# State chain in one operation over all heads, y products with 64 output rows, and the first two triangular systems by halves

## The chip, the cores and the metric

The kernel runs on one core of a Trainium2 chip. The core has a matrix engine (TensorE, PE in the profile), a vector engine (VectorE, DVE), an activation engine (ScalarE, ACT), a general engine (GpSimd, POOL), and SyncE (SP), which here issues the DMAs. PE writes to eight PSUM banks; DVE and ACT read PSUM, POOL does not. The metric is the time of one launch in device microseconds. All data are 32-bit floats.

## The reference

The first part is a linear recurrence with a matrix state per batch and head (4 batches, 8 heads, 768 time steps, head size 40); the second is a soft mixture of experts over its output. Cut to what matters:

```python
for t in range(768):                       # state: (4, 8, 40, 40), from zero
    y[:, :, t] = einsum('bhd,bhde->bhe', r_t, state)
    Sa    = einsum('bhde,bhe->bhd', state, a_t)
    state = state * w_t[:, :, None, :] - einsum('bhd,bhe->bhde', Sa, b_t)
    state = state + einsum('bhd,bhe->bhde', v_t, k_t)
x = y as (3072, 320)
logits = x @ phi                           # 32 slots, 4 for each of 8 experts
d = softmax(logits, over tokens);  c = softmax(logits, over slots)
slot_out[e] = relu((d.T @ x)[e] @ w1[e]) @ w2[e]      # 320 -> 1024 -> 320
out = c @ slot_out
```

## The kernel before

Time is cut into 12 steps of 64 time steps (`st`, `NST`), and each step into two halves of 32 (`q`). Two steps are a super-step (`ss`, 6 of them). The 8 heads lie in three groups (`u`; 3, 3 and 2 heads, so 120, 120 and 80 partitions), and each group has the 4 batches. Inside a half the recurrence is a triangular system of size 32 for each batch and head; its inverse T is worked out for a whole super-step at once, for the 4 halves, 4 batches and 8 heads: 128 systems, one on each partition after a transpose.

- **Preparation** of a step: `scan_s`, `scan_k`, `scan_c` build running products of w (scans on DVE, 1.8 us each) and scale k, b and a (three wide multiplies of 768 columns, in most steps on POOL); `bda_at` lays out the scaled a by heads; `lgram` makes the entries of the triangular systems (tile `lls`), `gram` the products for the chain (`qls`, `q0s`), `kbtok` and `ctok_of` transposes.
- **Solve** of a super-step: `solve_in` transposes the systems on DVE into `lt_a` and copies them to `n_a` on ACT; `solve_step`, 30 times, is a multiply into a temporary (`tmp_r`) and an addition into `n_a`; `solve_out` transposes `n_a` on DVE into T (`tts`, of which there is one tile; `lt_a` and `n_a` exist once too). `JP` splits the columns between POOL (up to `JP[ss]`) and DVE (the rest): 3 of 32 on POOL in super-step 0, 7 in super-step 1, all on POOL in the other four.
- **Chain** of a step, the part that is sequential from step to step: `chain_g` (products with the state and with v, or with the first half's result; copied from PSUM to `gss` by ACT), `chain_u` (T times G, negated by ACT into `vus`), for each half and each group; then `chain_s`, the new state.
- **Output** of a step, one step later: `y_vut`, `y_sd` (transposes), `y_p` (masked products), `y_y` (the y products, in 32 output rows each, and the multiply into `xs`), then the slot logits and sums (`slots_*`) every second step, and after the last step the experts.

The order of the work is not the order of the calls. Each call is recorded by `Plan` as an operation with its engine and the tiles it touches; consecutive matmuls into one bank with one tiling become one operation. `schedule` gives each a priority (the longest path behind it, moved by 300 times an entry of the string `SHIFT`) and places operations one after the other on the engines by assumed costs; the program is emitted in that order. Where a gap on PE of over 900 ns is expected, `filler` puts dummy matmuls into it (lines 553 and 557), which keep PE busy. `WIN`, `WIN0` and `PRO` give the order in which the calls of a step are recorded. In the trace, all instructions but the fillers carry line 1276, or 1528 and 1534 at both ends.

Of the kernel before, what the change touches and what calls it, by code (L numbers as in the profile page):

```python
# [11 lines left out]
ALU = mybir.AluOpType  # L12
# [17 lines left out]
JP = (3, 7, 32, 32, 32, 32)  # L30
# [80 lines left out]
class Engine:  # L111
# [29 lines left out]
    r"To')E:@oFhXL;s4JO+UO>!OQ!i0IXai!OO0zcwufU0#!2HOO,:!JPOTvYRS|N~[;tR7NkW~!7z]u2Hzu_O&B|%~!R_gLQOXOS#!OF|CO:H6NNQ!c"  # L141
    r"ODIObM^(|f7M#|a+&lAQ<1-Z60-(A]6YO!EM[#!OI!!!$!#OO#!+YTRGu^N+SIK!PECP.mgSdK{<yxftQMI[RFN$cD7-|4S/LM1R+OwvOqe9|kP$"
    r"FvkOTj>[OLqOrEXsRUU|KFO!NE]-$|NSOOT7?vIB|[spk!6FXGAd<QOD$OOHXBnJEI[Z?<ZrP?|2~F|U7O%FS$NgPEV~eAgQ6K9|R65%3|OMI[_C"
    r"OJH|S*DdXv|EN<tC<]P1N|NxRh=B>$XXr|nF){JO:Yk!|z#&.TT^#P#*LVf2^OVkQQ@LHjy!qZN!7G|eoPJ7b|!!$$!!$$!!^R8NjMO(JaXVdP]x"
    r"S]OBHQ!5JCD]=<!h<+Md~%KR:DOH!|oPv-HbO.!TSS9-OQ?IF*4nsN!>;NV!:[|$@H?>RON8OH0a4%|^|[|SQ6SAI/jWMUJ+a|]dCfp3QBOBr!$N"
    r"Ol|7O_xO!vNOS]c?MdO3Oxz*#{zSHPY|D%L~IYP%_9-P<y@OuO,U_4&/7W917HEPwuBs$yhxybQ5iAPyL_P<N#QKNB93#O~EU]@UEiy|$~ea2t:>"
    r".1K|NhE|O|!M.R<z|uRj8Q:l###[UkC!O%[O|J|sOmx~UUQ##cdNl~|W{bkHwH#!P:w#<UX?pNb||JTHQ|MtJ]D09PKK%U#!HlpYOO@K!mMFOqG`"
    r"oJ{LLP!GP/ZOQqH|KOybssS'!NFG!O#!!HON41c!!!=2:+&Rn|e|9YRA{AOnS=Rvi~!#IAE%M)I!DcSZd|esTEecD0N:|On~###xM|J|X|5|>Ow*"
    r"Q'RZO/|M|OV$UOfOjefV%Q[P|oO##|9G5(R.UaP4NGdOvK_PYMMgKLRE'|OOF([OOD|#DPSRN[|<1zjQzQ?ZA|XOVY|O|j]lzMlO7SO@+&MH*;3W"
    r",VH+.4c4F>bup,KU7HD0r!=!OH9qp?uaMyK`{7g{ADgUOO#`UwLj|NrNVGbLP|[7|NOZ;!d%{a~i/YQZeOO2/QwORQczKq3J/G;_Jc!;I@ITTF(C"  # L150
    r"HU(k!~!?&04G#=#_F>vH!H!XPGj,?|OUOdg]de_Y!BLOXmO[A%!Lb0JgW7V))6TO|QOQA#vM!8&rBOxzO90Q|||zp~XhOur|S|J!{T:=PsM+SOZ6"
    r"jKKD+k||NaKF~k]_X]!G6*9P$OB538'F$M3Rhc=#+KOfOuJQwOq7ppOPOTJ:n@jOLLOQg[-Dm%OfC|.O7K#<X$!!VMJO0;@XfdOO2GQo!O'PqZoe"
# [28 lines left out]
class Plan:  # L181
# [34 lines left out]
    def record(self, eng, method, a, k):  # L216
# [7 lines left out]
        if eng == "PE" and self.open is not None:  # L224
            o = self.open
            if o.mode == mode and isinstance(out, VAP) and (o.banks == {out.bank} or self.gather and o.gather) and o.tag == self.tag:
                new = False
        if new:
            o = Op()
            o.eng, o.calls, o.acc, o.banks, o.mode, o.kind, o.dma, o.tag, o.alt = eng, [], {}, set(), mode, method, 0, self.tag, None  # L230
# [7 lines left out]
        for i, x in enumerate(aps):  # L238
            w = i == 0
            if isinstance(x, VAP):  # L240
                if x.bank not in o.banks:
                    o.banks.add(x.bank)
                    x.bank.ops.append(o)
# [417 lines left out]
def rwkv_softmoe(ctx, tc, kb, b2, aa, ww, rr, vv, vq, consts, phi, w1, w2, out):  # L661
# [78 lines left out]
    with ExitStack() as ac:  # L740
# [27 lines left out]
        gss = Ring(part(4, 120) for _ in range(4))  # L768
# [22 lines left out]
        xts = Ring(mid[:, 4 * HD + 512 * i:4 * HD + 512 * i + 512] for i in range(2))  # L791
        wts_t = Ring(space(512) for _ in range(2))
# [17 lines left out]
        def cols(u):  # L810

            return slice(u * 480, u * 480 + 4 * NHU[u] * D)

        def grp(u, b):
            o = u * 480 + b * NHU[u] * D
            return slice(o, o + NHU[u] * D)

# [71 lines left out]
        def kbtok(st, u):  # L889
# [7 lines left out]
            nc.scalar.copy(kbks[st][:, cols(u)], tp[:, 0:4 * n])  # L897
# [66 lines left out]
        def solve_step(ss, i):  # L964
# [573 lines left out]
```

## Time and profile before

| what | value |
|---|---|
| time, median of 3 runs | 428.48 us (427.35 to 433.18) |
| profiled execution, its own time | 428.65 us |
| its span, from first to last instruction | 426.9 us |
| granted TensorE clock, mean | 0.972 |
| busy: PE / DVE / ACT / POOL | 365.3 / 261.7 / 221.6 / 246.7 us |
| weight loads (PEld) | 312.1 us |
| matmul instructions | 9473 |
| DMA traffic | 59.33 MB, mean 139 GB/s |

PE's busy time counts dummy matmuls as well. A matmul of 32-bit floats is two instructions (with two weight loads), so counts in the trace are twice those of calls in the code. Because nearly all instructions share one line, groups are told apart by engine, operation, tiles and shapes: `32*32 32x40` is a product with 32 contracted rows, 32 output rows and 40 columns (U and G of the chain), `128*32 128x40` the y products, `120*128 120x192` those of `y_p`; a `128xN` TENSOR_TENSOR from `wt` to `wt` is a solve step, one of `120x768` a multiply of the preparation.

### The profile page before, as it was taken

How to read it: one execution, taken by the hardware profiler on the slowest of the kernel's cores; microseconds unless marked ns; L12 is line 12 of the kernel's file. 1: busy time of each engine (PE TensorE's matmuls, PEld its weight loads, DVE VectorE, ACT ScalarE, POOL GpSimd, SP SyncE). 2: the span in 40 equal slices, each digit the busy share in tenths (PEclk: the TensorE clock that was granted, in tenths of full speed). 3: DMA queues.
4: the chain of work that ended last, by engine and by line, in shares of the span. 5: the costliest groups of instructions: out<-in, count | busy, mean ns of one | idle time of the engine just before them, and what ended most of it. 6: DMA issues, size and time to landing. Idle time of an engine off the chain costs nothing.

```text
span 426.9 us, 21521 instructions
## 1 busy us (share of the span) xinstructions
PE 365.3 (86%) x9473; PEld 312.1 (73%) x9473; DVE 261.7 (61%) x558; ACT 221.6 (52%) x637; POOL 246.7 (58%) x410
## 2 busy tenths in 40 slices
PE   0598996899999998899997999999979889889930
PEld 0587985799978897677896889987868778734830
DVE  6689989799958448854597644735542534642130
ACT  1550544964357654977437566597544266522130
POOL 6457964958499999889978899288820000110000
PEclk9999999999999999999998999999989999989985
DMA  8989232134222444404353324387675465881077
GB/s 197 248 221 271 59 81 60 55 101 128 77 77 76 133 123 129 128 19 137 89 177 102 100 68 114 103 259 245 185 213 162 132 174 175 245 257 64 3 174 195
DMA packets 36894, 59.33 MB, mean 139 GB/s; under 512 B 4849, under 2 KB 26465, under 8 KB 36801
## 3 DMA queue, kind: packets, MB, share of 16 engines
q1 hardware_dynamic: 36801, 57.96, 48.0%
q8 instruction: 74, 1.21, 1.2%
q14 instruction: 19, 0.16, 0.1%
HBM read 54.01 MB, written 3.93 MB: 136 GB/s over the span
## 4 chain that ended last, share of the span: by engine, by line
PE 60%; DVE 11%; ACT 8%; POOL 7%; issue 7%; DMA 3%; SPq 1%; DVEq 0%; ACTq 0%
PE ps L1276 53%; DVE wt L1276 9%; POOL wt L1276 7%; ACT wt L1276 5%; PE ps L557 4%; DMA bm_t<-in_consts_dram 2%; PE ps L553 2%; ACT mem L1276 2%; DMA mem<-in_rr_dram 1%; SPq L1276 1%; DVE mem L1276 1%; DVE old L1276 0%; DVE ps L1276 0%; ACT mid L1276 0%; DVE old_r L1276 0%
## 5 line engine op out<-in xcount | busy, mean ns | idle before, releaser
L1276 POOL TENSOR_TENSOR wt<-wt 128x30 f32<-128x30 f32 (+23 forms) x360 | 182.0, 506 | 53.3 <-ACT wt L1276 27.4
L1276 PE MATMUL ps<-wt,wt 128*32 128x40 f32 (+9 forms) x4200 | 136.7, 225 | 22.9 <-ACT wt L1276 15.9
L1276 PEld LDWEIGHTS ps<-wt,wt 128*32 128x32 f32 (+7 forms) x4200 | 116.2, 118 | 36.7 <-issue 24.8
L1276 DVE TENSOR_TENSOR wt<-ps,cs_t 128x384 f32<-128x384 f32 (+6 forms) x132 | 63.4, 496 | 34.1 <-PE ps L1276 30.3
L1276 ACT ACTIVATE wt<-ps 32x120 f32<-32x120 f32 (+1 forms) x288 | 70.2, 250 | 26.0 <-PE ps L1276 21.6
L1276 ACT COPY wt<-ps 128x120 f32<-128x120 f32 (+3 forms) x120 | 39.5, 350 | 61.7 <-PE ps L1276 59.0
L1276 PE MATMUL ps<-cs_t,wt 120*128 120x120 f32 (+5 forms) x496 | 67.5, 268 | 0.8 <-ACT wt L1276 0.3
L1276 ACT COPY mem<-ps 120x512 f32<-120x512 f32 (+6 forms) x99 | 46.0, 483 | 37.4 <-PE ps L1276 33.4
L1276 POOL TENSOR_TENSOR wt<-wt,wt 120x768 f32<-120x768 f32 x32 | 56.9, 1789 | 9.1 <-DVE wt L1276 5.7
L1276 PE MATMUL ps<-wt,mem 128*32 128x160 f32 (+4 forms) x592 | 62.2, 305 | 0.0
L1276 PEld LDWEIGHTS ps<-cs_t,wt 120*128 120x128 f32 (+5 forms) x496 | 50.1, 137 | 6.7 <-issue 2.3
L1276 PEld LDWEIGHTS ps<-wt,mem 128*32 128x32 f32 (+4 forms) x592 | 52.1, 151 | 1.9 <-issue 0.4
L1276 DVE TENSOR_TENSOR_SCAN wt<-wt,wt 120x780 f32<-120x780 f32 x24 | 44.8, 1870 | 2.7 <-DMA wt<-in_ww_dram 2.5
L1276 DVE TENSOR_TENSOR wt<-wt 128x27 f32<-128x27 f32 (+25 forms) x100 | 38.8, 388 | 2.0
L1276 PE MATMUL ps<-mem 32*32 32x40 f32 (+2 forms) x1040 | 33.7, 230 | 3.8 <-issue 2.0
L1276 POOL MEMSET mem<- 128x2048 f32 x1 | 1.8, 1805 | 58.7 <-DVE mid L1276 58.7
L1276 ACT ACTIVATE wt<-wt,bm_t 120x768 f32<-120x768 f32 (+1 forms) x36 | 28.6, 861 | 11.2 <-issue 6.0
L1276 DVE TENSOR_TENSOR ps<-ps,wt 120x480 f32<-120x480 f32 (+1 forms) x30 | 18.0, 606 | 26.0 <-PE ps L1276 21.8
L1276 PE MATMUL ps<-wt 32*32 32x40 f32 x1536 | 25.7, 205 | 5.5 <-issue 1.6
L1276 PEld LDWEIGHTS ps<-wt 32*32 32x32 f32 x1536 | 19.2, 109 | 13.1 <-issue 5.8
L1276 DVE STREAM_TRANSPOSE wt<-wt 128x1024 f32<-128x1024 f32 x12 | 24.6, 2095 | 2.4 <-POOL wt L1276 2.2
L1276 PEld LDWEIGHTS ps<-mem 32*32 32x32 f32 (+2 forms) x1040 | 18.8, 108 | 9.0 <-issue 4.3
(91 smaller groups left out, 314.4 us busy)
## 6 DMA issues: line engine op xcount, KB each, us to landing
wt<-in_w_dram SPq DMA_DIRECT2D x16, 640.0 KB
wt<-in_kb_dram SPq DMA_DIRECT2D x36, 240.0 KB
wt<-in_w_dram SPq DMA_DIRECT2D x16, 512.0 KB
wt<-in_ww_dram SPq DMA_DIRECT2D x12, 366.6 KB
mem<-in_rr_dram SPq DMA_DIRECT2D x36, 120.0 KB
wt<-in_vv_dram SPq DMA_DIRECT2D x24, 160.0 KB
wt<-in_rr_dram SPq DMA_DIRECT2D x96, 40.0 KB
wt<-in_aa_dram SPq DMA_DIRECT2D x30, 120.0 KB
```

What stands on the lines that cost most here:

```text
L553: self.nc.tensor.matmul(bank, src, src, start=True, stop=True)
L557: self.nc.tensor.matmul(bank[i:i + 32], src[r, 0:32], src[r], start=True, stop=True)
L1276: nc.vector.memset(one_f, 0.0)
```

## The change

`chain_g` and `chain_u` handle all 8 heads in one operation: G is one PSUM bank with 320 columns and one copy, U goes to two banks, batches 0 and 1 into one that ACT negates, batches 2 and 3 into one that DVE negates, 32 x 320 at a time. For that, v, `vus` and `kbks` are stored with the heads of a batch side by side (`tok`, `head`). `y_y` makes 64 output rows with one matmul instead of twice 32. Super-steps 0 and 1 (`QUICK`) are solved by halves, on DVE alone: 14 steps on the two 16 x 16 diagonal blocks together, then `solve_join`, which makes the off-diagonal block with two products on PE for each system (Y from the entries and the first block, copied by ACT; Z from Y and the second block; added on DVE). `JP` goes away; the other super-steps stay on POOL as they were. `SHIFT` has an entry for each operation of the new list (2,088 instead of 2,592). The string and the moves that follow from it are left out below.

```diff
-JP = (3, 7, 32, 32, 32, 32)
+QUICK = 2
...
-        gss = Ring(part(4, 120) for _ in range(4))
+        gss = Ring([part(4, HD)])
...
+        erow = mid[:, 0:512].rearrange("p (c h j) -> p c h j", c=4, h=H)
+        ysb = mid[:, 512:1536].rearrange("p (c h j) -> p c h j", c=4, h=H)
...
         def solve_in(ss):
             lt, n_t = lt_a, n_a
             nc.vector.transpose(lt.rearrange("p i t -> p t i"), lls[ss].rearrange("p c h t -> p t (c h)"))
...
+            if ss < QUICK:
+                nc.scalar.copy(n_t[:, 0:16, 0:16], lt[:, 0:16, 0:16])
+                nc.scalar.copy(n_t[:, 16:32], lt[:, 16:32])
+                nc.vector.memset(n_t[:, 0:16, 16:32], 0.0)
+                nc.vector.memset(n_t.rearrange("p i t -> p (i t)")[:, 0:1024:33], 1.0)
+            else:
+                nc.scalar.copy(n_t, lt)
+                nc.gpsimd.memset(n_t.rearrange("p i t -> p (i t)")[:, 0:1024:33], 1.0)
...
+        def solve_half(ss, i):
+            m = 15 - i
+            tv = tmp_r[i % 4][:, 0:2 * i * m].rearrange("p (h j t) -> p h j t", h=2, j=i)
+            nc.vector.tensor_tensor(tv, halves(n_a, 0, i, i, i + 1).broadcast_to([128, 2, i, m]),
+                                    halves(lt_a, i, i + 1, i + 1, 16).broadcast_to([128, 2, i, m]), ALU.mult)
+            nt = halves(n_a, 0, i, i + 1, 16)
+            nc.vector.tensor_tensor(nt, nt, tv, ALU.add)
+
+        def solve_join(ss):
+            tt, ll = tts.put(ss), lls[ss]
+            nc.vector.transpose(erow.rearrange("p c h j -> p j (c h)"), n_a[:, 0:16])
+            nc.vector.transpose(tt.rearrange("p c h t -> p t (c h)"), n_a.rearrange("p s t -> p t s"))
+            for x in range(2):
+                yp, zp = bank("jy"), bank("jz")
+                cs = [(c, h) for c in (2 * x, 2 * x + 1) for h in range(H)]
...
+                        nc.tensor.matmul(q(yp, c, h)[r], ll[r, c, h], erow[r, c, h], start=True, stop=True)
+                nc.scalar.copy(ysb[:, 2 * x:2 * x + 2, :, 0:16].rearrange("p c h j -> p (c h) j"),
+                               yp[:, 0:256].rearrange("p (x j) -> p x j", j=16))
...
+                        nc.tensor.matmul(q(zp, c, h)[r], ysb[r, c, h], tt[r, c, h, 16:32], start=True, stop=True)
+                to = tt[:, 2 * x:2 * x + 2, :, 16:32].rearrange("p c h t -> p (c h) t")
+                nc.vector.tensor_tensor(to, to, zp[:, 0:256].rearrange("p (x t) -> p x t", t=16), ALU.add)
...
-        def chain_g(st, u, q):
+        def chain_g(st, q):
             vu, sold = vus[st], st_of.get(st)
             gp = bank(f"gps{st}")
             if sold is not None:
+                for u in range(NU):
+                    n, o = NHU[u] * D, H0[u] * D
+                    for b in range(B):
+                        nc.tensor.matmul(gp[32 * b:32 * b + 32, o:o + n], ahs[st][0:n, B * u + b, 32 * q:32 * q + 32],
+                                         sold[0:n, grp(u, b)], start=(u == 0), stop=False, skip_group_check=True)
+            for h in range(H):
...
-            gs = gss.put(6 * st + 3 * q + u)
-            nc.scalar.copy(gs[:, 0:n], gp[:, 0:n])
+            nc.scalar.copy(gss.put(2 * st + q), gp[:, 0:HD])
...
+            up = [bank(f"ups{st}"), bank(f"upt{st}")]
...
+                    nc.tensor.matmul(up[b // 2][r, h * D:(h + 1) * D], tt[r, c, h, :], gs[r, h * D:(h + 1) * D],
                                      start=True, stop=True)
...
             for b in range(B):
-                nc.scalar.activation(vu[ur, grp(u, b)], up[32 * b:32 * b + 32, 0:n], AF.Copy, scale=-1.0)
+                x, y = vu[ur, b * HD:b * HD + HD], up[b // 2][32 * b:32 * b + 32, 0:HD]
+                if b < 2:
+                    nc.scalar.activation(x, y, AF.Copy, scale=-1.0)
+                else:
+                    nc.vector.tensor_scalar(x, y, -1.0, None, ALU.mult)
...
-                bx = [(b, slice(32 * x, 32 * x + 32), slice(64 * (b % 2) + 32 * x, 64 * (b % 2) + 32 * x + 32))
-                      for b in (2 * i, 2 * i + 1) for x in range(2)]
+                bx = [(b, slice(64 * (b % 2), 64 * (b % 2) + 64)) for b in (2 * i, 2 * i + 1)]
...
                 sol = solve_items(st // 2 + 1)
-                n = WIN["n0"][0 if st else 1]
+                n = WIN["n0"][0] if st else len(sol) // 2
```

More of the change, by code (lines that the diff above doesn't have):

```diff
@@ L225, in record @@
             o = self.open
-            if o.mode == mode and isinstance(out, VAP) and (o.banks == {out.bank} or self.gather and o.gather) and o.tag == self.tag:
+            if o.mode == mode and isinstance(out, VAP) and (list(o.banks) == [out.bank] or self.gather and o.gather) and o.tag == self.tag:
                 new = False
@@ new lines, in halves @@
+        def halves(t, j0, j1, t0, t1):
+            row, o = t.ap[0][0], t.offset + 32 * j0 + t0
+            return bass.AP(tensor=t.tensor, offset=o, ap=[list(t.ap[0]), [528, 2], [32, j1 - j0], [1, t1 - t0]])
+        def solve_half(ss, i):
[5 more added lines that the diff above has]
+            nc.vector.tensor_tensor(nt, nt, tv, ALU.add)
@@ L1000, in chain_g @@
             if sold is not None:
-                for b in range(B):
-                    nc.tensor.matmul(gp[32 * b:32 * b + 32, 0:n], ahs[st][0:n, B * u + b, 32 * q:32 * q + 32],
-                                     sold[0:n, grp(u, b)], start=True, stop=False)
-            for j in range(nh):
+                for u in range(NU):
+                    n, o = NHU[u] * D, H0[u] * D
+                    for b in range(B):
+                        nc.tensor.matmul(gp[32 * b:32 * b + 32, o:o + n], ahs[st][0:n, B * u + b, 32 * q:32 * q + 32],
+                                         sold[0:n, grp(u, b)], start=(u == 0), stop=False, skip_group_check=True)
+            for h in range(H):
+                u = h // 3
                 for b in range(B):
@@ L1251, in solve_items @@
         def solve_items(ss):
+            if ss < QUICK:
+                return ([lambda: solve_in(ss)] + [lambda i=i: solve_half(ss, i) for i in range(1, 15)]
+                        + [lambda: solve_join(ss)])
             return ([lambda: solve_in(ss)]
@@ L1501, in layouts @@
     v = np.asarray(inputs["v"]).reshape(B, H, NST, 2, 32, D)
-    vv = np.concatenate([v[:, H0[u]:H0[u] + NHU[u]].transpose(2, 3, 4, 0, 1, 5).reshape(NST, 2, 32, -1)
-                         for u in range(NU)], axis=3)
-    vv = vv.reshape(NST, 64, -1)
+    vv = v.transpose(2, 3, 4, 0, 1, 5).reshape(NST, 64, -1)
     vq = v[:, :, :, 0].transpose(2, 0, 3, 1, 4).reshape(NST, 128, HD)
```

120 lines of the change are left out of this document (55 added, 65 removed).

## The prediction

> **What bounds the kernel now.** I read the page's busy times first, then the table by stage (cut at the events named below), then the order of time at the cuts, then the groups by line inside a stage.
>
> ```profile
> span 426.9 us, 21521 instructions
> PE 365.3 (86%) x9473; PEld 312.1 (73%) x9473; DVE 261.7 (61%) x558; ACT 221.6 (52%) x637; POOL 246.7 (58%) x410
> ...
> 15.76:66.59 50.83, 45.64 (x986) 42.72 (x987) 42.73 (x92) 19.56 (x41) 36.50 (x69) 1.00 0.62 168
> 66.59:118.20 51.61, 46.86 (x1301) 42.12 (x1301) 47.97 (x100) 31.29 (x89) 35.63 (x70) 1.00 0.29 80
> 118.20:314.38 196.18, 184.45 (x5210) 157.72 (x5210) 120.92 (x238) 126.06 (x379) 164.76 (x260) 0.99 0.44 129
> 314.38:364.32 49.94, 46.32 (x1367) 40.96 (x1367) 19.19 (x52) 25.29 (x85) 0.00 (x0) 0.97 0.57 168
> ...
> sum 426.90, PE 24.73 PEld 22.30; mean PE 3.53 PEld 3.19
> ...
> sum 426.90, PE 17.41 PEld 16.46; mean PE 2.49 PEld 2.35
> ```
>
> The columns of a stage are its length, then busy time and count of PE, PEld, DVE, ACT and POOL, clock, DMA share, GB/s. The two sums are those of lines 557 and 553 alone: dummy matmuls of `filler`, issued where PE was expected to be idle. PE's 86% thus holds 42.1 us of nothing. By stage: in the first two stages DVE is 84% and 93% busy while PE runs fillers and fetches; from 118 to 314 PE (94%) and POOL (84%) are close to full together; after 314 POOL is done. So the first 118 us belong to DVE, the next 196 to PE and POOL.
>
> ```profile
> 22.50 2.10 DVE L1276 STREAM_TRANSPOSE wt<-wt 128x1024 f32<-128x1024 f32 x1
> 24.64 1.14 ACT L1276 COPY wt<-wt 128x96 f32<-128x96 f32 x2 [1.46 <-DVE wt L1276]
> 63.09 1.21 DVE L1276 TENSOR_TENSOR wt<-wt 128x75 f32<-128x75 f32 x5
> 64.41 3.93 DVE L1276 STREAM_TRANSPOSE wt<-wt 128x1024 f32<-128x1024 f32 x2
> 66.59 0.78 PE L1276 MATMUL ps<-wt 32*32 32x40 f32 x63 [1.60 <-DVE wt L1276]
> 111.82 4.07 DVE L1276 STREAM_TRANSPOSE wt<-wt 128x1024 f32<-128x1024 f32 x2
> 118.20 0.35 PE L1276 MATMUL ps<-wt,wt 80*32 80x80 f32 x8 [0.87 <-DVE wt L1276]
> ```
>
> The reader is to see two solves here. System 0 goes in with the transpose at 22.50, comes out at 64.41, and the first U product of the state chain starts at 66.59, waiting for it. System 1 goes in right behind it and comes out at 111.82; step 2's chain, which needs it, moves on at 118. Both solves are on the path that sets the end.
>
> **Term 1: systems 0 and 1 by halves, on DVE.**
>
> ```profile
> L1276 DVE TENSOR_TENSOR wt<-wt 128x27 f32<-128x27 f32 (+13 forms) x54 | 20.6, 381 | 1.2
> L1276 DVE TENSOR_TENSOR_SCAN wt<-wt,wt 120x780 f32<-120x780 f32 x4 | 8.5, 2114 | 0.0
> ...
> L1276 DVE TENSOR_TENSOR wt<-wt 128x23 f32<-128x23 f32 (+11 forms) x46 | 18.2, 396 | 0.8
> L1276 DVE TENSOR_TENSOR_SCAN wt<-wt,wt 120x780 f32<-120x780 f32 x5 | 9.0, 1798 | 0.1
> ...
> 22.50:66.60 44.10, 38.91 (x811) 36.13 (x809) 40.40 (x87) 16.71 (x37) 30.81 (x66) 1.00 0.56 154
> 66.60:116.00 49.40, 45.52 (x1290) 40.97 (x1291) 45.79 (x97) 30.32 (x89) 34.63 (x67) 1.00 0.30 84
> ...
> L1276 DVE TENSOR_TENSOR wt<-ps,cs_t 128x256 f32<-128x256 f32 x24 | 9.7, 419 | 2.2 <-PE ps L1276 2.0
> L1276 DVE COPY wt<-ps 128x320 f32<-128x320 f32 x12 | 5.5, 489 | 2.2 <-PE ps L1276 2.1
> L1276 ACT COPY wt<-ps 128x320 f32<-128x320 f32 x24 | 9.9, 428 | 15.5 <-PE ps L1276 15.1
> ```
>
> From 22.5 to 116 DVE is busy 86.2 of 93.5 us (92%). Removed: its 54 and 46 solve operations, 38.8 us (POOL's share beside them, too, which frees POOL and shortens nothing by itself). Added: 14 steps x 2 operations x 2 systems = 56 operations of 2 x i x (15-i) = 28 to 112 elements. The row at 63.09 shows dependent ones of 75 elements and fewer follow each other every 0.24 us; the group mean is 0.38. I take 0.30: 16.8 us, with 13.4 and 21.3 as ends. The joins add two half transposes (half of 2.1, so 2.1 together), four additions of 256 columns at 0.42 (1.7), some clearing (0.3), and the chain of steps 0 and 1 adds its DVE negations, 2 x 2 x 2 of 320 columns at 0.49 (3.9). Together 24.8 in, 38.8 out: 14.0 less, at 92% fill 15 us of time, with 10 and 19 at the ends.
>
> Beyond that, the nine scans (17.5 us in the rows above) and the masks are partly work ahead for later steps. The shorter dependent chain (28 operations instead of 60) lets the first U product move up more than DVE's total does, and look-ahead work can slide into the stage where DVE has 38% free. All of the second stage's scans, 9.0 us, is the most; I take 5. Term 1 is -20, between -9 and -29.
>
> The join's PE part: 4 x 128 instructions for each system.
>
> ```profile
> 140.34 0.65 PE L1276 MATMUL ps<-wt 32*32 32x40 f32 x48
> ...
> L1276 PEld LDWEIGHTS ps<-wt 32*32 32x32 f32 x1536 | 19.2, 109 | 13.1 <-issue 5.8 <-ACT wt L1276 4.5 <-ACT mid L1276 0.7
> ```
>
> At 0.65/48 = 13.5 ns each that is 1.7 us a pass, 6.9 a system. In system 0 it lies where PE runs fillers now; what counts is its latency, a half transpose, four passes, an addition: about 8.5 us, so that system 0 needs 8.4 for its steps and 8.5 here, beside other DVE work, where it takes some 38 now (25.8 to 64.4). In system 1 it takes PE time in a stage where PE is 91% busy, fillers included; cover gone, it costs 6.9.
>
> **Term 2: the middle.** Per step, U goes from six groups of matmuls to two. The PEld row just above shows 13.1 us of idle time ahead of its 72 U groups (12 steps x 6), 0.18 each; in the eight steps between 118 and 314, 32 groups fewer are 5.8 us of PE. G's three groups per half become one likewise, which I leave at nothing. Against this stand the y products.
>
> ```profile
> 104.20 0.41 PE L1276 MATMUL ps<-mem 120*32 120x120 f32 x8
> 104.43 0.40 PE L1276 MATMUL ps<-wt,wt 128*32 128x40 f32 x24
> 104.64 0.41 PE L1276 MATMUL ps<-mem 120*32 120x120 f32 x8
> ...
> L1276 PE MATMUL ps<-wt,wt 120*96 120x96 f32 x192 | 19.8, 252 | 0.7 <-issue 0.6
> ...
> L1276 PE MATMUL ps<-wt,wt 80*96 80x64 f32 x96 | 10.3, 250 | 0.2 <-DVE mem L1276 0.2
> ```
>
> One half of one group, 8 + 24 instructions in four column groups, takes 0.44 us (104.20 to 104.64), 13.7 ns each. With 64 rows there are 4 + 12 in two column groups. If the count sets the time, it is 0.22 and the eight steps save 8 x 1.15 = 9.2 us. But the two gram rows say that a product with 96 output rows costs the same with 64 moving columns (10.3/96 = 107 ns) as with 96 (19.8/192 = 103): the weight columns set it, not the moving ones. At 103/96 ns a column less the groups' tails, an estimate of 54 ns for 64 weight columns, two at a time: 6 x 54 + 2 x 100 = 0.52 us, which is 0.46 a step more, 3.7 in eight. I take this end, since those rows are nearest.
>
> By the Trainium skill ("TensorE: Matmul & The Clock Gate", LDWEIGHTS) a weight load goes by its columns, P/1.2 ns, 53 for 64; with 40 moving columns that speaks against the wider output, as the gram rows do. Its "TensorEngine Tiling (Array Packing)" (Tiling Modes) says likewise two tiles for 64 columns where 32 have four. By these sentences alone the y term would be the same +3.7.
>
> ACT loses 24 small activations a step for 4 wide ones and six copies for two, DVE gains 4 x 0.49 = 2.0 us a step; with 62% and 64% busy there, neither is on the path. POOL's four full solves stay. Term 2 is -5.8 + 3.7 = -2, between -15 and +4.
>
> **Term 3: the last two steps.**
>
> ```profile
> L1276 ACT ACTIVATE wt<-ps 32x120 f32<-32x120 f32 x192 | 49.5, 261 | 16.7 <-PE ps L1276 13.6
> ...
> L1276 ACT ACTIVATE wt<-ps 32x80 f32<-32x80 f32 x96 | 21.8, 227 | 9.3 <-PE ps L1276 8.0
> ```
>
> After 314 the chain runs with fillers between its parts. A half ends now with 8 x 0.261 + 4 x 0.227 = 3.0 us of negations in a row on ACT; then with two of 0.43 on ACT beside two of 0.49 on DVE, 1.0. Four halves save 8 us at most; half of it lies beside y products, so -4.
>
> Sum: -20 - 2 - 4 = -26 on the profiled execution's 428.65 us (0.2 above the median of 428.48, so no correction): **402 us**.
>
> **Rivals.**
> *POOL keeps the pace.* Its third solve needs system 1 out and the inputs of steps 4 and 5. If that look-ahead stays where it is, the four POOL solves start only term 1's least (9 us) earlier, and nothing but the tail comes on top: 428.65 - 9 - 4 = 416. For it: 164.76 of 196.18 us busy; against it: the other 31 us are slack. Chance 0.17.
> *The port.*
>
> ```profile
> 47.28 0.33 DVE L1276 TENSOR_TENSOR wt<-wt 128x187 f32<-128x187 f32 x1
> 47.68 4.81 POOL L1276 TENSOR_TENSOR wt<-wt,wt 120x768 f32<-120x768 f32 x2
> 50.92 1.78 DVE L1276 TENSOR_TENSOR wt<-wt 128x187 f32<-128x187 f32 x1
> ```
>
> The same DVE form takes 0.33 us alone and 1.78 beside POOL's multiplies. If the new steps meet these at the old rate, an operation costs 0.38 and DVE saves 5 us less: 407. Chance 0.08. The Trainium skill ("SBUF — State Buffer", Who interferes with whom) calls this an exclusive lock on a shared port pair; the two rows agree.
> *More comes.* All the look-ahead slides, y goes by the count, the tail gains 6: -29 - 11 - 6 = -46, 383. PE allows it: 365.3 - 42.1 + 13.8 for the joins + 15.8 before its first matmul + 16.7 after its last is 370. Chance 0.18.
> *Slower: the chain loses its three-way overlap.* Now one group's copy runs beside the next one's matmuls. As one operation, G (88 instructions, 1.5 us), copy 0.43, U (64, 1.1), negation 1.0, twice, then the state (some 4) make 12 us, and each of five visits to PE can wait 2 us behind other work: 22. A step has 196.18/8 = 24.5, so it fits; if the visits cost 3.3 us each, every step is 4 us longer, 9 steps +36, less 20: 445. It decides from 2.5 us a visit. Chance 0.04.
> *It doesn't bring the start forward*, because step 2's inputs, not system 1, come last: 422 to 430. Chance 0.06.
>
> **Numbers.** Forecast 402 (392 to 412) 0.47; the rest as above. A measurement of this kernel tells about 2% from no change. Below 420: 0.47 + 0.18 + 0.08 + 0.15 of the POOL case: 0.88; within 2%: 0.08; slower: 0.04. The range for 8 in 10 takes in the POOL and port cases and part of the larger gain: 386 to 418.
>
> **What would show it.** Right: first U product (32*32, 40 columns) near 50 instead of 66.59 (25.8 + 8.4 + 8.5 and some 7 of other DVE work); step 2's chain near 98 instead of 118; POOL's third solve starting with it; some 42 us of fillers shrinking below 25; a y half at 0.5 us. Wrong: a y half at 0.22, PE gaps between G and U in the middle, or POOL idle after 118 for lack of grams.

## The result, and the profile after

The changed kernel takes 416.98 us (median of 4 runs, 416.13 to 422.90) where the kernel before, timed beside it, takes 427.92 (4 runs, 426.25 to 433.18): a ratio of 0.975, 95% interval 0.9705 to 0.9796. The forecast of 402 has the sign right and the size wrong: the profiled run is 12.7 us shorter in its span, not 26. (Ratios leave disturbed executions out, medians and ranges don't; of one kernel below, the joins with longer products, only the profile of a disturbed one is at hand.) First the page of the changed kernel: span, busy times, granted clock in 40 slices.

```profile
span 414.2 us, 19908 instructions
...
PE 348.7 (84%) x8863; PEld 303.7 (73%) x8863; DVE 273.8 (66%) x570; ACT 168.0 (41%) x353; POOL 199.3 (48%) x289
...
PEclk9999579995999999999999999999999999999965
```

Before, the clock row was full over the whole front; here it is 0.5 in the slice of 41 to 52 us, 0.7 in the next, and 0.5 again at 93 to 104 us. The table by stage, cut at 59.4, 112.3 (the U products of steps 0 and 2) and 309.9 (step 10), has as columns length, then busy time and count of PE, PEld, DVE, ACT and POOL, clock, DMA share and GB/s:

```profile
59.40:112.30 52.90, 44.66 (x1621) 40.05 (x1613) 46.66 (x92) 19.69 (x38) 21.85 (x33) 0.87 0.21 60
112.30:309.90 197.60, 189.54 (x4693) 169.87 (x4692) 140.53 (x276) 94.53 (x197) 149.48 (x234) 1.00 0.49 141
309.90:414.20 104.30, 79.79 (x1542) 62.01 (x1541) 39.96 (x122) 31.76 (x80) 3.17 (x5) 0.91 0.58 164
```

The U products are good milestones. Step 2's came at 121.16 before and comes at 112.28, step 10's at 316.38 and 309.89, the span ended at 426.9 and 414.2. So the front gave 8.9 us (forecast 20), the eight steps between cost 2.4 (forecast a gain of 2), and the end gave 6.2 (forecast 4): -8.9 + 2.4 - 6.2 = -12.7.

These are three places in time, not quite the three terms, for the work between the milestones isn't the same. PE's 40-column y products between step 2's and step 10's U, before and after:

```profile
L1276 PE MATMUL ps<-wt,wt 128*32 128x40 f32 x896 | 16.5, 199 | 1.6 <-issue 1.6
```
```profile
L1317 PE MATMUL ps<-wt,wt 128*64 128x40 f32 x576 | 24.7, 224 | 0.0
```

896 of 1536 are seven steps' products, 576 of 768 are nine: two steps' y products moved out of the front into the stretch where PE is the bound, and two steps' masked products lie there more, too. In it `y_y` keeps PE busy for 43.6 us instead of 32.4 and `y_p` for 39.5 instead of 31.2, together 19.5 more, for 2.4 us more of time. The chain pays for most of it: its G and U products take 41.2 us of PE there instead of 54.6.

Where the front lost its gain is read from the order of time, first of DVE, then of PE. The bracket is the idle time ahead and what ended it; "issue" means that no instruction of another engine was waited for.

```profile
37.20 0.98 DVE L1317 STREAM_TRANSPOSE mid<-wt 128x512 f32<-128x512 f32 x1
...
39.51 1.78 DVE L1317 TENSOR_TENSOR_SCAN wt<-wt,wt 120x780 f32<-120x780 f32 x1
...
41.42 1.77 DVE L1317 TENSOR_TENSOR_SCAN wt<-wt,wt 120x780 f32<-120x780 f32 x1
...
43.50 3.08 DVE L1317 TENSOR_TENSOR_SCAN wt<-wt,wt 120x780 f32<-120x780 f32 x1
46.50 2.13 DVE L1317 STREAM_TRANSPOSE wt<-wt 128x1024 f32<-128x1024 f32 x1
...
51.76 0.42 DVE L1317 TENSOR_TENSOR wt<-wt,ps 128x256 f32<-128x256 f32 x1
```

```profile
38.33 1.56 PE L1317 MATMUL ps<-mid,wt 32*32 32x16 f32 x153 [1.01 <-DVE mid L1317]
44.84 1.58 PE L1317 MATMUL ps<-mid,wt 32*32 32x16 f32 x103 [4.95 <-issue]
...
49.79 1.91 PE L1317 MATMUL ps<-wt,mid 32*32 32x16 f32 x128
...
59.46 0.79 PE L1317 MATMUL ps<-wt 32*32 32x40 f32 x64
```

System 0's join begins at 37.20 and its addition ends at 52.18: 15.0 us for a latency that was forecast at 8.5. Three look-ahead scans stand on DVE ahead of the full transpose, and PE stops for 4.95 us in the middle of a pass after 153 short matmuls, with nothing to wait for. System 1's join has the same holes (2.37 us up to 94.74, 1.98 up to 98.62). The table in steps of 4 us shows the clock, in the last column but two:

```profile
40.00:44.00 4.00, 0.00 (x0) 0.00 (x0) 3.90 (x5) 0.18 (x1) 0.72 (x1) 0.52 0.87 225
44.00:48.00 4.00, 3.10 (x111) 2.69 (x111) 4.00 (x2) 1.19 (x3) 2.28 (x2) 0.50 0.05 12
48.00:52.00 4.00, 3.50 (x143) 3.11 (x144) 3.95 (x10) 4.00 (x7) 3.66 (x3) 0.50 0.62 166
52.00:56.00 4.00, 2.47 (x88) 2.10 (x88) 2.28 (x4) 2.87 (x6) 2.05 (x2) 0.50 0.18 47
56.00:60.00 4.00, 4.00 (x135) 3.79 (x138) 1.22 (x4) 0.78 (x3) 1.29 (x1) 0.85 0.09 28
```

The granted clock is 0.50 for some 17 us, from 40.15 to 57.22, and comes back only when PE is busy throughout. The Trainium skill ("TensorE: Matmul & The Clock Gate", What's actually happening) gives half clock after an idle window of some 3.4 us and full clock after a busy one. The return agrees (PE was busy without a break from 53.80 to 57.22); the fall doesn't, since it came 0.3 us into the hole, after 3.4 us of which PE was busy for 2.1. So this hole can have kept the clock down, but what brought it down lies ahead of it: the 1.01 us of waiting for the half transpose, or the short products themselves.

### The profile page after: what moved, and what is told of

Same layout as the page of the kernel before. It is cut to its first block, busy times and chain, and to the rows that moved or that the text cites. A ratio compares the mean times of both kernels' runs of the same rounds, so it can differ in the third digit from the quotient of the medians.

```text
span 414.2 us, 19908 instructions
## 1 busy us (share of the span) xinstructions
PE 348.7 (84%) x8863; PEld 303.7 (73%) x8863; DVE 273.8 (66%) x570; ACT 168.0 (41%) x353; POOL 199.3 (48%) x289
## 4 chain that ended last, share of the span: by engine, by line
PE 67%; issue 6%; DVE 6%; DMA 4%; POOL 2%; ACT 2%; SPq 0%; DVEq 0%; ACTq 0%; POOLq 0%
PE ps L1317 66%; DVE wt L1317 4%; POOL wt L1317 2%; DMA wt<-in_w_dram 1%; DMA wt<-in_rr_dram 1%; DVE mem L1317 1%; DMA wt<-in_ww_dram 1%; ACT wt L1317 1%; DMA wt<-in_kb_dram 1%; ACT mem L1317 1%; PE ps L552 0%; ACT mid L1317 0%; SPq L1317 0%; DVE mid L1317 0%; DVE old L1317 0%
## 5 line engine op out<-in xcount | busy, mean ns | idle before, releaser
L1317 POOL TENSOR_TENSOR wt<-wt 128x30 f32<-128x30 f32 (+14 forms) x240 | 132.7, 553 | 45.1 <-ACT wt L1317 24.0
L1317 PE MATMUL ps<-wt,wt 96*32 96x40 f32 (+8 forms) x3432 | 140.4, 238 | 2.1 <-DVE wt L1317 0.6
L1317 PEld LDWEIGHTS ps<-wt,wt 120*32 120x32 f32 (+7 forms) x3432 | 125.8, 129 | 11.8 <-issue 3.9
L1317 DVE TENSOR_TENSOR wt<-ps,cs_t 128x384 f32<-128x384 f32 (+5 forms) x132 | 62.8, 496 | 36.8 <-PE ps L1317 32.0
L1317 PEld LDWEIGHTS ps<-cs_t,wt 120*128 120x128 f32 (+5 forms) x496 | 52.2, 140 | 23.8 <-ACT wt L1317 17.7
L1317 ACT COPY wt<-ps 128x320 f32<-128x320 f32 (+1 forms) x72 | 32.9, 469 | 42.6 <-PE ps L1317 40.2
L1317 DVE TENSOR_SCALAR wt<-ps 32x320 f32<-32x320 f32 x48 | 23.6, 492 | 11.7 <-PE ps L1317 10.9
L1317 ACT ACTIVATE wt<-ps 32x320 f32<-32x320 f32 x48 | 20.5, 426 | 25.0 <-PE ps L1317 22.6
L1317 PE MATMUL ps<-wt 32*32 32x40 f32 x1536 | 19.5, 199 | 3.9 <-ACT wt L1317 2.4
L1317 ACT COPY mid<-ps 128x512 f32<-128x512 f32 (+3 forms) x24 | 12.0, 507 | 25.1 <-PE ps L1317 25.0
```

The source lines that it names most:

```text
L1317: nc.vector.memset(one_f, 0.0)
```

## Experiments

Theories. *Fetch*: the joins' many short matmuls outrun the delivery of PE's instructions. *Clock*: the holes halve PE's clock for what follows. *DVE's order*: the scans ahead of the transpose make the join late. *Fixed pace*: whatever the front gains, the middle takes back. All kernels keep the changed kernel's order of instructions unless said otherwise. A ratio is against the kernel before on the same chip; "stretch" is the time from step 2's U to step 10's U in one profiled execution. It holds seven steps' y products in the kernel before, with or without 64 rows, and without halves, and nine in all others, so only kernels with the same number are compared by it.

| kernel | first U | step 2's U | stretch | time, median (range) | ratio, 95% |
|---|---|---|---|---|---|
| before | 66.59 | 121.16 | 195.2 | 427.92 (426.25-433.18) | 1 |
| changed | 59.46 | 112.28 | 197.6 | 416.98 (416.13-422.90) | 0.975 (0.9705-0.9796) |
| wide joins | 55.73 | 107.17 | 201.8 | 417.91 (415.76-420.29) | 0.9721 (0.9648-0.9795) |
| wide joins, three times | 56.87 | 106.72 | 207.1 | 421.03 (420.11-422.56) | 0.9785 (0.971-0.9861) |
| wide joins, dummies | 53.73 | 103.22 | 203.2 | 415.40 (414.44-418.50) | 0.9764 (0.9615-0.9912) |
| scans cut | 58.96 | 110.35 | 198.8 | 421.10 (414.33-423.40) | 0.9786 (0.9485-1.0087) |
| wide joins, scans cut | 49.64 | 96.48 | 206.8 | 413.62 (412.23-418.22) | 0.9725 (0.9519-0.9931) |
| whole fetches less | 55.75 | 107.59 | 195.6 | 415.33 (412.00-422.56) | 0.9638 (0.9541-0.9735) |
| whole fetches less, scans cut | 53.80 | 107.10 | 197.9 | 413.61 (409.35-416.59) | 0.9591 (0.9508-0.9674) |
| whole fetches less, dummies | 55.31 | 106.22 | 197.2 | 410.74 (408.94-411.66) | 0.9552 (0.9513-0.9591) |
| the same, half a fetch more | 53.75 | 105.87 | 201.6 | 414.20 (410.44-418.40) | 0.9596 (0.9484-0.9708) |
| joins' products longer | 61.28 | 112.95 | 197.9 | 419.40 (413.87-421.04) | 0.968 (0.9545-0.9815) |
| newly planned | 55.67 | 103.46 | 196.6 | 412.04 (407.32-417.10) | 0.9538 (0.943-0.9647) |
| without halves | 69.39 | 132.10 | 188.7 | 432.41 (428.45-440.30) | 1.0041 (0.9972-1.0109) |
| y in 32 rows | 60.60 | 114.14 | 207.2 | 430.11 (424.79-436.79) | 0.9949 (0.9909-0.999) |
| y in 32 rows, filled up dearly | 61.08 | 114.92 | 223.8 | 454.59 (454.29-456.90) | 1.0579 (1.0482-1.0677) |
| y in 32 rows, filled up cheaply | 61.44 | 115.51 | 213.4 | 440.14 (439.42-453.25) | 1.0173 (1.0069-1.0278) |
| before, y in 64 rows | 69.98 | 123.48 | 191.9 | 426.52 (423.64-428.24) | 0.9932 (0.9894-0.997) |

### Wide join products, once and three times

```
- for c, h in cs: for b in range(B):        # 64 a pass, 16 columns each
-     matmul(q(yp, c, h)[r], ll[r, c, h], erow[r, c, h])
+ for b in range(B):                        # 4 a pass, 256 columns each
+     matmul(yp[r, 0:256], ll[r, 2 * x, 0], erow[r, 2 * x:2 * x + 2])
```

The same for z. One head's weights serve for all heads here, so this is a simplified join, for looking and not for use; the passes' place and dependences stay. In the second kernel the wide products are issued three times.

> The changed kernel in the same order of operations, but each of the join's four passes is 4 products of 256 columns instead of 64 of 16 (it leaves out the separate entries for 15 of 16 systems, so the off-diagonal blocks are not the true ones): 8 instructions a pass instead of 128. Theory A (the burst of short products outruns instruction fetch, PE stands still, and the granted clock falls to half after it): the 4.9 us hole in PE at 39.9 us and those of 1.6 to 2.4 us at the other passes go, the clock between 40 and 60 us rises from 0.5 to 0.6 to near 1, the first U product moves from 59.5 to about 50, step 2's from 112 to about 102, and the kernel takes 405 to 410 us. Theory B (DVE is still what binds the first 110 us): the first U product moves by 1 to 2 us, the kernel by less than 3 us (414 to 418).

> The same with every wide product issued three times over: 24 instructions a pass instead of 128, but about as much PE time as in the changed kernel (3 x 0.44 us against 1.5). Theory A: like the kernel with single wide products within 2 us, since it is the number of instructions that hurts. Rival (the join's PE time itself is what delays the chain): like the changed kernel, 415 to 418 us.

```profile
44.00 1.46 PE L1329 MATMUL ps<-cs_t,wt 120*128 120x120 f32 x6 [3.76 <-ACT wt L1329]
48.90 1.07 PE L1329 MATMUL ps<-wt,mid 32*32 32x256 f32 x8 [3.44 <-DVE wt L1329]
...
55.73 0.47 PE L1329 MATMUL ps<-wt 32*32 32x40 f32 x29
```

The order of time of PE with wide joins: the issue holes of the join are gone, first U comes 3.7 us and step 2's 5.1 us earlier. Now PE waits for ACT and DVE (the full transpose behind the scans), and the clock still falls. So the short products cost the front 4 to 5 us. But the time stays: the stretch grew by 4.2 us, with three times the products by 9.5. (The threefold kernel's front is as early, 106.72 at step 2's U; that it is 3 us slower than the single one, not within 2, comes from the stretch.) This was the question for all that follows.

### Dummies in the holes; scans cut; both

```
+ WARM = {154: 14, 177: 12, 282: 7, 320: 7, 404: 8, 410: 6}   # dummies ahead of these operations
```
```
+ SHORT = (97, 100, 151)      # these three scans work on columns 0:8 only
```

> The kernel with wide join products, order unchanged, and 56 dummy matmuls (128x128, into free bank columns) put ahead of the six instructions at which PE stood idle 1.6 to 3.8 us for ACT or DVE around the two joins, so that PE isn't idle there. Theory 'clock' (holes of 2 to 5 us bring the granted clock to 0.50 for some 10 us, and PE's work around the joins then takes twice as long): the clock stays at 0.95 or more between 40 and 104 us; PE was busy some 3, 7.5 and 6 us in the three stretches at half clock, so half of that, about 8 us, comes back by step 2: first U 55.7 -> 53 to 54, step 2's U 107.2 -> 99 to 102. Theory 'DVE's order' (the holes come from waits for DVE, which the clock doesn't change): the clock rises but the first U stays within 1 us of 55.7 and step 2's U comes within 2 us of 107. Theory 'the middle takes it back': whatever the front gains is gone by step 10 and the time stays at 414 to 419; if it carries, 409 to 412.

With the dummies the clock is full from 20 to 120 us, and step 2's U comes 4 us earlier than with wide joins alone, the first U 2.0. So the clock is worth 4 us at step 2, less than the 5 to 8 that were expected of it, and the stretch grew again. (A second pair of kernels, further down, gives 1.4 us.)

> The changed kernel, same order, with three look-ahead scans of DVE (1.77, 1.77 and 3.08 us at 39.5 to 46.5 us, for later steps) cut to 8 columns each; their results for those steps are left out. They stand ahead of the full transpose that system 0's join waits for. Theory 'DVE's order': the transpose starts at 41 instead of 46.50, z and the addition follow, and the first U comes 4 to 5 us earlier (59.5 -> 55); step 2's U 112.3 -> 107. Theory 'fetch and clock': PE is held by its own hole of 4.95 us up to 44.8 and by half clock behind it, so the first U moves by 0 to 2 us. The term as forecast (DVE's total sets the front): 5.3 us less DVE work gives 5 us at step 2. At the end 412 if carried, 415 to 418 if the middle takes it back.

```profile
44.49 1.58 PE L1322 MATMUL ps<-mid,wt 32*32 32x16 f32 x103 [5.23 <-issue]
...
49.44 1.91 PE L1322 MATMUL ps<-wt,mid 32*32 32x16 f32 x128
...
58.96 0.79 PE L1322 MATMUL ps<-wt 32*32 32x40 f32 x64
```

PE of the kernel with the scans cut: the full transpose starts at 40.73 instead of 46.50, but the issue hole is still there, and the first U moves by 0.5 us, step 2's by 1.9. *DVE's order* alone doesn't bind, and 4.8 us less of DVE's work (three scans of 0.15, 0.16 and 1.48 us instead of 1.78, 1.77 and 3.08) aren't 5 us less of time; *fetch* and *clock* hold PE.

> Both: wide join products and the three scans cut to 8 columns (their results are left out), same order. If the joins' fetch holes and the scans ahead of the transpose are the two things that kept system 0's join at 17 us instead of 8.5, the first U comes at 50 to 52 (the forecast's mark was 50) and step 2's U at 101 to 103. If only one of them binds, the first U stays at 54 to 56. Time 408 to 412 if the front's gain is carried to the end, 414 to 419 if it is taken back as with wide join products alone (first U -3.7, end -0.3).

```profile
43.28 0.63 PE L1334 MATMUL ps<-wt,mid 32*32 32x256 f32 x8 [1.89 <-DVE wt L1334]
...
49.64 0.55 PE L1334 MATMUL ps<-wt 32*32 32x40 f32 x38
```

With both, the first U stands at 49.64 and step 2's at 96.48: even before the forecast's marks of 50 and 98. Neither edit alone does it. And yet the span is only 1.3 us shorter than the changed kernel's: 9.2 us of the 15.8 are gone by step 10, the rest in the last two steps and the tail, where the clock was 0.87 and 0.78 in stretches that had 1.00.

### The same join, each product longer

```
- matmul(q(yp, c, h)[r], ll[r, c, h], erow[r, c, h])               # 16 columns
+ matmul(yp[r, 16 columns of heads h to h + 3], ll[r, c, h], erow[r, c, h:min(h + 4, H)])
```

> The changed kernel in its order and with its count of instructions; each of the joins' narrow products takes the moving columns of up to three heads more along (64 columns instead of 16), and the next head's product writes over what doesn't belong there, so that the values are the same as in the changed kernel. A pass of 64 matmuls then takes PE some 1.7 us instead of 0.9, near the 2 to 2.4 us for which PE stood idle within system 1's passes. Theory 'fetch and clock': the holes of 2.37 and 1.98 us in system 1's join shrink below 1 us, the clock between 90 and 104 us stays at 0.9 or more (0.5 before), and step 2's U comes at 108 to 111 instead of 112.28; the hole of 4.95 us in system 0's join, beside a DMA share of 0.87 to 0.97, stays above 3 us; the stretch stays at 197 to 199 us, since no instruction is added, and the time is 412 to 416. If the products' own time counts: step 2's U at 113 to 116, time 418 to 421.

```profile
42.24 2.43 PE L1329 MATMUL ps<-mid,wt 32*32 32x64 f32 x103 [2.81 <-issue]
...
96.22 1.10 PE L1329 MATMUL ps<-mid,wt 32*32 32x48 f32 x80 [1.59 <-issue]
...
99.83 1.92 PE L1329 MATMUL ps<-wt,mid 32*32 32x48 f32 x83 [1.86 <-issue]
```

A miss. The holes in system 1's join shrink from 2.37 and 1.98 to 1.59 and 1.86 us, not below 1, and that in system 0's to 2.81, not above 3; the clock in system 1's join is better (1.00, 0.74 and 0.83 at 94 to 106 us where it was 0.60, 0.50 and 0.62), but the longer products use that up: step 2's U at 112.95, 419.40 us (413.87 to 421.04). The hole in system 0's join opens after 153 matmuls as before, though these took 2.18 us instead of 1.56. With exact joins I have no version that is faster than the changed kernel.

### Where the gain went: the places of the fetches

The wait tables of PE, cut to the stretch (total, times, longest), first of the changed kernel, then of wide joins with scans cut:

```profile
PE ps L1317 <- issue: 2.5, 4, 0.8
```
```profile
PE ps L1334 <- issue: 7.8, 6, 2.1
```

There is no wait for POOL to speak of (0 and 1.2 us), which speaks against a pace that POOL sets; the instructions of this stretch are the same, in the same order. What differs is how many stood ahead of them, and when they come. The page of the changed kernel has a queue for instructions (packets, MB), and so has that of the kernel below with 768 records less in each join:

```profile
q8 instruction: 69, 1.13, 1.2%
```
```profile
q8 instruction: 63, 1.03, 1.0%
```

69 packets for 2 x 8863 records of PE and PEld are 257 a packet; 1536 records less are 6 packets less. So instructions come 256 at a time, and the constant 256 in the planner's `FETCH` says the same. If the order was fitted to where these packets fall, a change of the count by a part of 256 shifts all that follows.

```
+ each pass: the 4 wide products, then 12 of the old narrow ones (16 instead of 64)
```

> Wide join products, four a pass, followed by 12 of the old narrow ones (they write the same values again), so that a pass has 16 matmuls instead of 64: over a system PE has 192 matmuls less, 768 instruction records, a whole multiple of the 256 that the planner in the kernel counts as one fetch. Order unchanged. Wide products alone (240 matmuls less, not a multiple) had step 2's U 5 us earlier, but the stretch from there to step 10's U took 201.8 us instead of 197.6, with 'issue' holes. Theory 'fetch phase' (the order fits the places where fetches fall, and a shift of these opens new holes): the stretch takes 197 to 199 us again; step 2's U at 107 to 109, step 10's at 305 to 307, time 411 to 414. Theory 'fixed pace' (what starts earlier waits later, for inputs or POOL): the stretch takes 201 to 204, step 10's U at 309 to 311, time 415 to 418.

> The same with the three look-ahead scans cut to 8 columns (results left out). With wide products and the scans cut, but not a multiple of 256 records less, step 2's U came at 96.5, 15.8 us earlier than in the changed kernel, and the end 1.3 us earlier: the stretch from step 2's to step 10's U took 206.8 us. 'Fetch phase': 197 to 200 us from about 97 on, step 10's U at 294 to 298, time 399 to 404: then the front was worth its 15 us. 'Fixed pace': step 10's U stays at 302 to 306, time 411 to 415.

> The first of these with 64 dummy matmuls (again 256 records) in the holes around the joins; nothing is left out. With 56 dummies and the other count the clock at 40 to 104 us went up (0.5 to 0.83 before) and step 2's U came at 103.2, but the stretch to step 10's took 203.2. 'Fetch phase': step 2's U at 103 to 105, the stretch 197 to 200, step 10's U at 301 to 304, time 407 to 411, the best yet. 'Fixed pace': step 10's U at 306 to 308, time 413 to 417.

The narrow ones write 3 of a pass's 16 blocks anew; the others keep the simplified join.

The stretch is 195.6, 197.9 and 197.2 us, with issue holes of 2.7, 1.5 and 3.5 us. It is 198.8 with the scans cut alone and 197.9 with longer products, two kernels that keep the changed kernel's count; the four whose count isn't whole had 201.8, 203.2, 206.8 and 207.1. *Fixed pace*, as it was put, falls: step 10's U came at 303.19 in the first and 303.40 in the third, 6.7 and 6.5 us ahead of the changed kernel. A weaker form of it stays open: wide joins with scans cut also reach step 10's U at 303.24, from a front 10 us earlier, and no kernel here has both whole packets and such a front. The second was meant to, but its front didn't come at 97 but at 107.10, beside a clock of 0.67 at 50 to 60 us and 0.51 at 70 to 80, where the earlier kernel with scans cut had 1.00; its step 10's U (304.95) and its time are what *fixed pace* expected of it. So the scans are worth 0.5 or 10.7 us at step 2's U, and why isn't settled.

```profile
span 409.6 us, 18627 instructions
...
PEclk9999999999999999999999999999998999999975
```

The third, with dummies, has the lowest median: its page has a full clock all through the front, and 410.74 us. Its step 2's U is 1.4 us ahead of the first's (106.22, not the 103 to 105 expected), so full clock, less the dummies' own time, is worth 1.4 us here and was worth 4.0 above.

```
- for c, h in cs[:3] for b in range(B)
+ for c, h in cs[:11 if ss + x == 0 else 3] for b in range(B)     # 32 matmuls, 128 records more
```

> The best version so far (410.7 us: wide and 12 narrow products a pass, 64 dummies) with 32 narrow products more in one pass of system 0's join: 0.4 us of PE's time, 128 records, half a fetch; nothing else. Theory 'fetch phase': the front moves by less than 1.5 us, but new 'issue' holes open behind it: stretch from step 2's to step 10's U 200 to 207 instead of 197.2, time 414 to 419. If the theory is wrong: 410 to 412.

```profile
PE ps L1339 <- issue: 5.4, 5, 1.5
```

The control: half a packet more and nothing else. The front stays (53.75 and 105.87), the stretch goes from 197.2 to 201.6 us with 5.4 us of issue holes instead of 3.5 (and 1.6 us more of waiting for ACT), and the time from 410.74 to 414.20, all as *fetch phase* had it. The ranges of the times overlap, and the profiled execution, 416.45 us, is among the longer ones of this kernel; the verdict rests on the stretch, and on its fitting the rest: 195.6 to 198.8 us in the six kernels of this order whose count is whole, 201.6 to 207.1 in the five others.

> The changed kernel with wide join products (4 a pass) and a new order, for which the planner knows them: it expects less fetch stall (2.9 us instead of 17.3) and puts in 86 groups of dummies instead of 40. Nothing is left out. If the front is worth its time when holes and half clock are both planned away: first U at 52 to 56, step 2's at 97 to 103, stretch 197 to 200, time 402 to 409. If there is a fixed pace behind it: 410 to 416.

Wide joins (simplified as above), known to the planner, and a new order: step 2's U at 103.46, a little past its mark, the stretch at 196.6. The profiled run took 407.32; the median, 412.04 of four runs spread over 10 us, is no better than the version with dummies. Both are faster than the changed kernel, with the simplified join; neither is a version to use.

### Without the halves

```
- QUICK = 2
+ QUICK = 0
+ JP = (3, 7, 32, 32, 32, 32)      # systems 0 and 1 as in the kernel before; a new order
```

> The changed kernel without its first part: systems 0 and 1 are solved as before by DVE and POOL together (7 and 3 of 32 rows on POOL), the chain in one operation and the 64-row products stay. The order is planned anew, and less finely than the two others. If the halves are what brings the front forward, the first U comes at 64 to 70 and step 2's at 117 to 124 as before the change, and the time is 421 to 428: halves worth 5 to 10 us. If the chain in one operation and the wider y products bring the change's gain, first U late and yet 414 to 419. If they cost (the forecast had the y products at +3.7 us): 428 to 434.

First U 69.39, step 2's at 132.10 (past its mark; the clock was 0.66 at 70 to 80 us), 432.41 us, its span 12.7 us over the changed kernel's. Against the kernel before it gains nothing as a whole, but by place it does: from step 2's U on it is faster, with seven steps' y products in the stretch as there (188.7 us for 195.2, and 106.1 for 110.5 behind it). Its front, with the same solves, is 10.9 us later and takes that back; the order was planned with less search than the other two. So the change's second and third part gain some 6.5 and 4.5 us here, and the 12.7 us are an upper figure for the halves: what they are worth alone isn't isolated.

### The y products

The edit of the changed kernel; the kernel before gets the reverse one.

```
- bx = [(b, slice(64 * (b % 2), 64 * (b % 2) + 64)) for b in (2 * i, 2 * i + 1)]
+ bx = [(b, slice(32 * x, 32 * x + 32), slice(64 * (b % 2) + 32 * x, ...)) for b in ... for x in range(2)]
```

> The changed kernel in the same order, but with the y products in 32 output rows as before. The trace of the changed kernel shows 0.58 us for a y half of a group of three heads, the one before 0.43 to 0.44, so 64 rows cost about 0.76 us of PE a step. If PE is what binds the middle: 5 to 9 us faster than the changed kernel (408 to 412). If twice the instructions make up for it in fetch holes: no change or slower (416 to 422). If POOL or the chain binds: within 2 us.

> The kernel before in its own order, with nothing changed but the y products in 64 output rows. By the same price: 5 to 9 us slower than before (433 to 437) if PE binds, within 2 us if not, and faster (about 420) if the number of instructions is what sets the price of a y product.

The groups of the y products, first in the kernel before, then in it with 64 rows (busy, mean ns | idle ahead and what ended most of it):

```profile
L1276 PE MATMUL ps<-wt,wt 128*32 128x40 f32 x1536 | 27.6, 200 | 2.1 <-issue 2.1
...
L1276 PE MATMUL ps<-mem 120*32 120x120 f32 x352 | 18.1, 270 | 0.2 <-issue 0.2
...
L1276 PE MATMUL ps<-mem 80*32 80x80 f32 x176 | 6.9, 236 | 3.2 <-DMA mem<-in_rr_dram 1.7 <-issue 1.5
```
```profile
L1292 PE MATMUL ps<-wt,wt 128*64 128x40 f32 x768 | 32.8, 223 | 0.0
...
L1292 PE MATMUL ps<-mem 120*64 120x120 f32 x176 | 18.2, 286 | 0.0
...
L1292 PE MATMUL ps<-mem 80*64 80x80 f32 x88 | 7.7, 253 | 0.0
```

Busy time goes from 52.6 to 58.7 us, +6.1 in twelve steps or +4.1 in eight: the forecast's +3.7. But the idle time ahead goes from 5.5 to 0, PE's issue waits, fillers apart, from 9.1 to 1.1 us, and the kernel becomes 0.7% faster, not slower. In the changed order 32 rows cost 9 us by the ratios and 12 by the spans, with 27.8 us of issue waits instead of 16.8. That run also shifted the fetches, so two more kept them in place with repeated matmuls, 256 records a step:

> The changed kernel with the y products in 32 output rows as before the change, and with 20 (step 0: 32) repeated first matmuls a step, so that a step has 64 matmuls, 256 instruction records, more: whole fetches. Without that filling up (2064 records more, not a multiple of 256) the 32-row form had given 430 us. Theory 'weights' (a 64-row half costs more PE time than it saves, the forecast's +3.7 us in eight steps): the 32-row form is the cheaper one when the places of the fetches are kept: stretch from step 2's to step 10's U 195 to 198 us, time 412 to 417. Theory 'records' (twice the matmuls outrun the fetch wherever they lie): the stretch takes 202 to 208, 'issue' holes over 12 us, time 422 to 430.

> As the last 32-row run, but the 20 (step 0: 32) matmuls that fill a step up to whole fetches are narrow (40 moving columns, spread over the four column groups, some 0.3 us a step) instead of the 120-column ones, which alone had cost PE 45 us. 'Weights' (a 64-row half costs PE more than it saves): PE's time in the real y products 54 us instead of 59, stretch from step 2's to step 10's U 194 to 199 us, time 411 to 418. 'Records' (twice the matmuls outrun the fetch wherever they lie): stretch 202 to 208, 'issue' holes over 12 us as with the 32-row form without filling (27.8), time 420 to 430.

```profile
PE ps L1336 <- issue: 35.4, 28, 5.2
```

The first failed as a price of y: its filling, 120 columns wide, cost PE 45 us (99.2 us busy in these products). The second's filling still costs 1 us a step where 0.3 was meant (40.7 us busy in the row of 40-column products instead of 28.1), so its time says little, but not its issue waits: 35.4 us, with packets in place, and a stretch of 213.4 us, some 204 without the filling's busy time. The two have the same number of records in the same places, and in the stretch the long filling leaves 5.6 us of issue waits, the short one 16.3. *Records* holds in this order: twice the matmuls outrun their delivery, also with packets in place. In the order of the kernel before, which was planned for 32 rows, they cost 0.7%.

## Why the prediction was wrong

**What bounds the kernel**: held in the middle, where PE is busy 189.54 of 197.60 us. In the front DVE is as full as forecast (46.66 of 52.90 us in the second stage), but its total doesn't set the time: 4.8 us less of it moved step 2's U by 1.9.

**Term 1** (-20, measured -8.9) is the step that failed, and in it the join's latency. System 0's halves came as worked out: 26.8 to 35.0 us, 8.2 for 8.4. The join took 15.0 us for 8.5, and that is 6.5 of the 9.5 by which the first U missed its mark of 50; the rest is a start 1.0 us late and 9.5 us of other work where some 7 were allowed. "At 0.65/48 = 13.5 ns each that is 1.7 us a pass" took the pace of 48 matmuls in a row for 256; the burst stopped after 153. It also counted PE's passes as the latency: with wide joins and scans cut, where they take some 2 us in place of 6.9, the join still takes 9.7 (36.50 to 46.25), for the full transpose and the addition stand in DVE's order behind other work. The sentence on DVE's total at 92% fill had no place for a PE that is late and at half clock. That the marks (50 and 98) were within reach is shown, with the simplified join, by wide joins with scans cut; that fetch and clock held them off, by wide joins (-5.1 at step 2) and dummies (a further 4.0, or 1.4). The price of 0.30 us an operation was right by luck: system 0's 28 took 0.25 each (6.9 us), system 1's, partly beside POOL's multiplies, 0.38 (10.7). The working also took for granted that what the front gains reaches the end. Under this fitted order a gain of 5 to 6 us at step 2's U reached step 10's where the places of the fetches stayed, and not where they moved; that a gain of 15 would is not shown.

**Term 2** (-2; the stretch went +2.4, with two steps' y products more in it, and -6.5 on seven steps in the kernel without halves). U: idle time ahead of its groups fell from 13.1 to 7.8 us in twelve steps, 3.5 in eight, for 5.8 forecast. G, "which I leave at nothing", was a term: its products keep PE busy for 28.0 us of the stretch instead of 37.0, and U's for 13.2 instead of 17.6. y: the price in busy time was right (+4.1 for +3.7), the count's effect was left out: with 32 rows the changed kernel is 9 to 12 us slower. "I take this end" chose between weights and count; both act, one on PE's busy time, the other on its delivery.

**Term 3** (-4, measured -6.2 from step 10's U to the end): right in sign, a half of the 8 us was taken and three quarters came, but one step's larger masked products have left this place too (6.1 us instead of 9.1). No run here isolates the negations.

**Rivals.** *POOL keeps the pace* named 416, and 416.98 came, but not by its mechanism: POOL's third solve starts at 94.91 instead of 117.05, and PE doesn't wait for POOL in the middle. That the time lies near 416 is luck for it. *The port* came for system 1 alone, as above. *The chain loses its overlap* and *It doesn't bring the start forward* didn't come. *More comes* needed a front that carries to the end; its tail of 6 came. Among the other marks, the dummies fell to 9.0 us (below 25), a y half takes 0.58 us (0.5), and POOL starts before step 2's chain: all as forecast.

## What to carry to other kernels

Read the instruction queue of the page and the issue waits of PE before a pass of hundreds of short matmuls is priced by the pace of a few dozen: the count per microsecond has a limit of its own, and wider matmuls that cost PE more can still be faster. In a kernel with an order fitted to the chip, change the count of instructions by whole packets, or plan anew; otherwise an experiment's gain at one end is lost at places that have nothing to do with it. Before a stretch is compared between two orders, count what work it holds. When PE gets a new wait of a few microseconds, price half clock on some 10 us around it (3 to 17 in the front of the changed kernel), or fill the wait.

## What the runs showed of the hardware

Instructions of PE arrive in packets of 256 (69 packets for 17726 records, 63 for 16190), and half a packet more ahead of an unchanged stretch made it 4.4 us longer. After 153 short matmuls in 1.56 us PE stood for 4.95 us beside a DMA share of 0.87, and for 2.37 us in the second join beside one of 0.04; whether the loads delayed the packet was not tried. A granted clock of 0.50 began 0.3 us into the first of these holes and lasted 17 us, while PE behind the hole was busy 3.10, 3.50 and 2.47 of 4 us; with wide joins and dummies in six waits it stayed at 1.00 up to 120 us.
